# Joint transfers for blocks 2 and 3, a new order for the stages of blocks 2 to 5, and later float64 work, in a kernel for attention and two gated layers

## The chip, the core and the metric

The kernel runs on one core of one Trainium2 chip. The metric is the device time of one execution in microseconds, as the median of several runs. For the kernel before it is 1256.46 us over three runs (1255.62 to 1256.68).

## The reference

A chunked attention feeds a layer of four experts, and that feeds a gated layer. Everything arrives in float32, except the three matrices of the gated layer, which come in float64 (they were scaled with a float64 factor).

```python
scores = scale * np.matmul(q_c, k_c.transpose(0, 1, 2, 4, 3))   # B, H = 4, 8; chunks of 64 of 576; D = 64
scores = scores - np.max(scores, axis=-1, keepdims=True)
attn = np.exp(scores)
attn = attn / (np.sum(attn, axis=-1, keepdims=True) + 1e-09)
x = np.matmul(attn, v_c)                                        # -> 2304 tokens x 512
for e in range(4):                                              # first layer: w1 512 x 1024, w2 1024 x 512
    out += p[:, e:e + 1] * (np.maximum(x @ w1[e], 0.0) @ w2[e])
g, val = out @ w_gate, out @ w_val                              # second layer: 512 x 1536
return (silu(g) * val) @ w_out                                  # 1536 x 512
```

## The kernel before

**Tiling.** The 2304 tokens make 18 blocks of 128 tokens, and three passes of six blocks (two halves of three blocks, 384 tokens each). Attention makes blocks 0 to 5 before the first pass; blocks 6 to 17 are made beside the matmuls of that pass. Every product of the layers is done in a split form: an operand is a rounded high part (`h`) and the rest (`l`), and three matmuls add up h·h, h·l and l·h. A weight's high part is a copy on ScalarE (ACT), its low part a subtraction on GpSimd (POOL), both at L105 and L106 (tile `w`).

**Sets of products.** A *set* is a square of 256 columns of the first matrices; the first layer has 16 sets a pass, the second 12 a pass, 84 in all. A set is made with seven half-size products (`PRODUCTS`, a Strassen scheme) out of sums of weights and sums of inputs, six matmuls each (L538 to L540, 384 columns). The first three sets have no sums of inputs yet and are made as twelve *plain* products (`next_plain`, tiles `plz`, `plw`, `plx`) of twelve matmuls each. Between the products stand the matmuls of the second matrices (`layer2`, tile `y`, L587 to L591, 512 columns).

**Blocks 0 to 5.** Each block a goes through stages, here with the names of their tiles: scores `s` (L238, 16 matmuls), maximum and difference on VectorE (DVE, `att_soft`, tiles `mx` and `e`), the exponential on ACT (`att_exp`), transposes `et` (L264), the sums of a row (`att_sums`, tiles `hs`, `sm`, `rs`), the products with the values `av` (L300), their scaling into `e` on DVE (L307), transposes `xt` and the split of the result (`att_out`: two high parts and a full copy `x` on ACT, L323 and L325; two low parts, on POOL or, for the last block of a half, on DVE straight from the PSUM tile, L109). TensorE runs its instructions in the program's order, so a stage that is not ready holds up all that stands behind it.

**Loads.** Queries, keys and values are loaded with 128 partitions of 2 KB each. Keys and values go into block-diagonal tiles (`kbd`, `vbd`): a transfer of 64 partitions for either head half, the rest being zeros that DVE and POOL write at the start. Transfers are issued on the queue of SyncE (SP) and, for a few, of ACT (L213 to L223). Eight semaphores serve all these transfers in turn, so a transfer is issued only when the one eight places earlier has landed; SP issues in order.

**Sets that are made beside the work.** From set 18 on a list of tasks turns the float64 weights into float32 and splits them (`convert`, `make_set64`, `make_wo`; the seven splits of such a set are tile `w_made`), and makes the sums of inputs of the next pass (`x_sums`). After each product `run_tasks(2)` lets every running task go on until it says `WAIT` or `STEP`, with two `STEP`s at most. A conversion allows two raw tiles (`loads`):

```python
while loads[0] == RAWS: yield WAIT
loads[0] += 1
nc.sync.dma_start(raw..., src)          # L402, 4 WAITs later the arithmetic begins
...
nc.gpsimd.tensor_tensor(out=neg, in0=neg, in1=low, op=ALU.mult)          # L423
nc.gpsimd.tensor_tensor(out=top or dst, in0=top, in1=neg, op=ALU.add)    # L424
loads[0] -= 1
```

`later(d, f)` calls f d products later. The weights of a coming product are loaded (or made) six products ahead (`LEAD`, `load_w`, L386). The end of a pass of the first layer transposes its sums once more (`turn_x1`, tile `x1t`, copied by ACT at L627), in the PSUM tiles that `y` uses too.

Of the kernel before, what the change touches and what calls it, by code (L numbers as in the profile page):

```python
# [19 lines left out]
P = 128  # L20
# [51 lines left out]
def attention_moe_gated(  # L72
# [125 lines left out]
    def place(a):  # L198
        return a % 4 if a < BLOCKS else a % 2

    def next_in_place(a):

        return next((b for b in range(a + 1, NS) if place(b) == place(a)), None) if place(a) < 2 else None

    def att_load(a):
        q = (at_p if a < 2 or a >= BLOCKS - 2 else first_p).tile([P, NPAIR, P], F32, tag="q", name=f"q{a}", bufs=2)
        k = kbd[place(a)]

        for h in range(2):
            b = slice(64 * h, 64 * h + 64)  # L210
            queue = nc.scalar if a < 2 and h == 0 else nc.sync
            if a < 2:
                queue.dma_start(q[b], qt[a, b])  # L213
            elif h == 0:
                (nc.scalar if a < 4 else nc.sync).dma_start(q, qt[a])
            queue.dma_start(k[b, h].rearrange("p i c t -> p (i c t)"), kt[a, b].rearrange("p i t -> p (i t)"))
        att[a] = {"q": q, "k": k}

    def att_load_v(a):
        v = vbd[place(a)]  # L220
        for h in range(2):
            b = slice(64 * h, 64 * h + 64)
            (nc.scalar if a < 2 and h == 0 else nc.sync).dma_start(  # L223
                v[b, h].rearrange("p i c d -> p (i c d)"), vt[a, b].rearrange("p i c d -> p (i c d)")
            )
        att[a]["v"] = v

    def att_ps(name, where):
        pool, tag = where
# [403 lines left out]
    with tc.manual_schedule():  # L633
# [17 lines left out]
        for i in range(4):  # L651
            pool = at_p if i < 2 else first_p
            kbd.append(pool.tile([P, 2, NPAIR, 2, CH], F32, tag=f"k{i}", name=f"kbd{i}", bufs=1))
            vbd.append(pool.tile([P, 2, NPAIR, 2, D], F32, tag=f"v{i}", name=f"vbd{i}", bufs=1))
# [6 lines left out]
        for i in range(4):  # L661
            for t in (kbd[i], vbd[i]):
                for h in range(2):
                    (nc.vector if t is kbd[0] or t is kbd[1] else nc.gpsimd).memset(t[64 * h : 64 * h + 64, 1 - h], 0.0)
            if i == 2:
# [14 lines left out]
        def where():  # L680
            count[0] += 1
            return spare[count[0] % len(spare)]
# [26 lines left out]
        def stages(*some):  # L709
            for stage, a, *w in some:  # L710
                if 0 <= a < BLOCKS:
                    stage(a, *w)

        for i in range(-1, BLOCKS + 1):
            if i >= HALF + 1:
                next_plain()
            stages((att_values, i - 1, where()))
            stages((att_scores, i + 1, where()))  # L720
            if i == HALF:
                stages((att_out, i - 1, where()))
            if i == BLOCKS:
                next_plain()
            stages((att_turn, i, where()), (att_soft, i + 1), (att_sums, i))
            if i != HALF:
                stages((att_out, i - 1, where()))
            stages((att_exp, i + 1))
            if i == 1:
                fetch_w1(1)  # L730
            elif i == 2:
                w_plain(0, ORDER[:2])
            elif i == 3:
                w_plain(0, ORDER[2:])
                fetch_w1(2)
                shares()
            elif i == 4:
                w_plain(1, ORDER)
            elif i == 5:
                w_plain(2, ORDER[:2])  # L740
                first_cm.close()
                w2_p = ctx.enter_context(tc.tile_pool(name="w2", bufs=7, reuse_waits="tile"))
                fetch_w2(0, 0)
                fetch_w2(0, 1)
                first_sums(0)

        del raw1[0], raw1[1]
        now[0] = -10
# [114 lines left out]
        for o in order:  # L863
# [129 lines left out]
```

## Time and profile before

| | |
|---|---|
| median of three runs | 1256.46 us |
| the profiled execution | 1255.25 us, span 1253.5 us |
| TensorE matmuls busy | 1238.6 us (99%) |
| weight loads / VectorE / ScalarE / GpSimd busy | 1119.6 / 678.4 / 519.1 / 580.8 us |
| granted TensorE clock | 1.00 over the span |
| DMA | 328.40 MB, 262 GB/s on average |

Times in the rows count from the start of the span; 1.75 us of the profiled execution lie outside it. Engine names: PE is TensorE, PEld its weight loads, SPq and ACTq the transfers that SP and ACT issue. In a row of a timeline the bracket at its end says how long the engine was idle before the instruction and what ended that.

### The profile page before, as it was taken

How to read it: one execution, taken by the hardware profiler on the slowest of the kernel's cores; microseconds unless marked ns; L12 is line 12 of the kernel's file. 1: busy time of each engine (PE TensorE's matmuls, PEld its weight loads, DVE VectorE, ACT ScalarE, POOL GpSimd, SP SyncE). 2: the span in 40 equal slices, each digit the busy share in tenths (PEclk: the TensorE clock that was granted, in tenths of full speed). 3: DMA queues.
4: the chain of work that ended last, by engine and by line, in shares of the span. 5: the costliest groups of instructions: out<-in, count | busy, mean ns of one | idle time of the engine just before them, and what ended most of it. 6: DMA issues, size and time to landing. Idle time of an engine off the chain costs nothing.

```text
span 1253.5 us, 19769 instructions
## 1 busy us (share of the span) xinstructions
PE 1238.6 (99%) x6730; PEld 1119.6 (89%) x6730; DVE 678.4 (54%) x1115; ACT 519.1 (41%) x1114; POOL 580.8 (46%) x573
## 2 busy tenths in 40 slices
PE   7999999999999999999999999999999999999998
PEld 6888888899898988898998999999999999999997
DVE  5766666666555767665565663443345433543333
ACT  4454434445344444544543442343334333433331
POOL 5454434577445556545574461144456332442321
PEclk9999999999999999999999999999999999999999
DMA  8588787799798888988899886667967676577541
GB/s 228 168 277 277 265 273 234 249 329 342 258 350 310 304 302 336 325 314 304 290 354 345 290 298 232 240 226 241 314 205 280 223 244 186 200 249 245 179 140 51
DMA packets 170660, 328.40 MB, mean 262 GB/s; under 512 B 18224, under 2 KB 44080, under 8 KB 170560
## 3 DMA queue, kind: packets, MB, share of 16 engines
q1 hardware_dynamic: 169760, 325.79, 75.2%
q10 hardware_dynamic: 768, 1.31, 0.4%
q8 instruction: 54, 0.88, 0.3%
q14 instruction: 46, 0.38, 0.1%
q0 software_dynamic: 32, 0.04, 0.0%
HBM read 235.31 MB, written 91.75 MB: 261 GB/s over the span
## 4 chain that ended last, share of the span: by engine, by line
PE 90%; DMA 4%; POOL 2%; DVE 1%; ACT 1%; issue 1%; SPq 1%; DVEq 0%; POOLq 0%
PE y L587 14%; PE y L591 14%; PE y L589 14%; PE lx L538 9%; PE lx L540 8%; PE lx L539 8%; PE lz L538 4%; PE lz L540 4%; PE lz L539 4%; PE lw L538 2%; PE lw L540 2%; PE lw L539 2%; PE s L238 1%; PE av L300 1%; DMA w<-w_made 1%
## 5 line engine op out<-in xcount | busy, mean ns | idle before, releaser
L587 PE MATMUL y<-w,hh 128*128 128x512 f32 x792 | 312.3, 394 | 1.5 <-ACT acc L627 1.5
L591 PE MATMUL y<-w,hl 128*128 128x512 f32 x792 | 312.0, 394 | 0.0
L589 PE MATMUL y<-w,hh 128*128 128x512 f32 x792 | 310.8, 392 | 0.2 <-POOL w L106 0.2
L106 POOL TENSOR_TENSOR w<-raw,w 128x256 fp32r<-128x256 f32 (+1 forms) x192 | 189.5, 1000 | 212.2 <-ACT w L105 184.4
L591 PEld LDWEIGHTS y<-w,hl 128*128 128x128 f32 x792 | 148.6, 188 | 32.9 <-POOL hl L109 0.3
L587 PEld LDWEIGHTS y<-w,hh 128*128 128x128 f32 x792 | 148.9, 188 | 29.8 <-ACT acc L627 2.0
L589 PEld LDWEIGHTS y<-w,hh 128*128 128x128 f32 x792 | 148.8, 188 | 28.0 <-POOL w L106 0.6
L109 POOL TENSOR_TENSOR hl<-sg,hh 128x384 fp32r<-128x384 f32 x72 | 78.2, 1091 | 182.0 <-ACT hh L513 130.1
L495 ACT ACTIVATE hh<-sum_p 128x384 fp32r<-128x384 f32 x90 | 47.2, 525 | 230.2 <-DVE sum_p L526 230.1
L526 DVE TENSOR_TENSOR sum_p<-lx,p 128x384 f32<-128x384 f32 x81 | 45.2, 557 | 175.5 <-PE lx L540 174.3
L608 DVE SCALAR_TENSOR_TENSOR acc<-y,prob,acc 128x512 f32<-128x512 f32 x126 | 91.5, 744 | 79.5 <-PE y L591 79.4
L106 POOL TENSOR_TENSOR w_made<-raw,w_made 128x256 fp32r<-128x256 f32 x84 | 68.1, 819 | 83.1 <-ACT w_made L105 67.9
L105 ACT ACTIVATE w<-raw 128x256 fp32r<-128x256 f32 (+1 forms) x192 | 90.3, 488 | 7.3 <-DVE raw L370 2.6
L496 DVE SCALAR_TENSOR_TENSOR hl<-sum_p,hh 128x384 fp32r<-128x384 f32 x90 | 58.3, 647 | 60.1 <-ACT hh L495 60.1
L522 ACT COPY u<-lx 128x384 f32<-128x384 f32 x81 | 38.6, 477 | 92.6 <-PE lx L540 92.6
L513 ACT ACTIVATE hh<-sg 128x384 fp32r<-128x384 f32 x72 | 38.0, 528 | 67.5 <-DVE sg L510 67.5
L526 DVE TENSOR_TENSOR sum_p<-lw,p 128x384 f32<-128x384 f32 x81 | 44.9, 554 | 37.5 <-PE lw L540 32.5
L423 POOL TENSOR_TENSOR neg<-neg,raw 128x512 f32<-128x512 f32 x24 | 32.0, 1333 | 70.4 <-DVE neg L421 26.4
L538 PE MATMUL lw<-b21h,w 128*128 128x384 f32 x162 | 54.9, 339 | 1.2 <-DMA w<-w 1.2
L538 PE MATMUL lz<-t1h,w 128*128 128x384 f32 x162 | 55.2, 340 | 0.2 <-DVE hl L496 0.2
L538 PE MATMUL lx<-t3h,w 128*128 128x384 f32 x162 | 55.0, 340 | 0.0
L538 PE MATMUL lx<-t2h,w 128*128 128x384 f32 x162 | 55.0, 340 | 0.0
(235 smaller groups left out, 2826.7 us busy)
## 6 DMA issues: line engine op xcount, KB each, us to landing
w<-w SPq DMA_DIRECT2D x567, 256.0 KB, 5.1
w<-w SPq DMA_DIRECT2D x96, 512.0 KB, 6.1
w<-w_made SPq DMA_DIRECT2D x84, 256.0 KB, 5.9
raw<-w SPq DMA_DIRECT2D x19, 512.0 KB, 4.5
raw<-wo SPq DMA_DIRECT2D x36, 256.0 KB, 4.7
raw<-w SPq DMA_DIRECT2D x32, 256.0 KB, 4.3
sums<-x SPq DMA_DIRECT2D x40, 192.0 KB, 3.9
xt<-sums SPq DMA_DIRECT2D x40, 192.0 KB, 4.7
```

Of the source, the lines that this page charges most:

```text
L105: nc.scalar.activation(h, src, AF.Copy)
L106: (lo or nc.vector).tensor_tensor(out=l, in0=src, in1=h.bitcast(F32), op=ALU.subtract)
L109: (eng or nc.vector).tensor_tensor(out=o, in0=a, in1=b, op=ALU.subtract)
L496: nc.vector.scalar_tensor_tensor(out=l, in0=src, scalar=0.0, in1=h.bitcast(F32), op0=ALU.max, op1=ALU.subtract)
L526: nc.vector.tensor_tensor(out=t, in0=ps, in1=snap.pop(name), op=ALU.add)
L538: nc.tensor.matmul(ps, w[:, 0, c], xh[:, k], start=f, stop=False, skip_group_check=True)
L539: nc.tensor.matmul(ps, w[:, 0, c], xl[:, k], start=False, stop=False, skip_group_check=True)
L540: nc.tensor.matmul(ps, w[:, 1, c], xh[:, k], start=False, stop=e, skip_group_check=True)
L587: nc.tensor.matmul(y, hh[:, c], w[:, 0], start=(j == 0), stop=False)
L589: nc.tensor.matmul(y, hh[:, c], w[:, 1], start=False, stop=False)
L591: nc.tensor.matmul(y, hl[:, c], w[:, 0], start=False, stop=(j == 3))
L608: nc.vector.scalar_tensor_tensor(out=sum_, in0=y, scalar=p, in1=sum_, op0=ALU.mult, op1=ALU.add)
```

## The change

Six edits. (1) Queries, keys and values of blocks 2 and 3 lie in joint tiles `q23`, `k23`, `v23`; one transfer (queries) or two (keys, values) bring both blocks, and the first weights (`raw1_0`) are fetched behind them. (2) The stages of blocks 2 to 5 and the first four plain products are written out in a new order. (3) `att_out` of the last block of a half copies `x` after the two low parts and not before them. (4) A conversion gives its raw tile free one product later. (5) `x_sums` stores its sums three products later. (6) `run_tasks` is left out for the first four products of a pass's first set.

```diff
-            yield WAIT
+            for _ in range(4):
+                yield WAIT
             for i, o in enumerate(("b11", "b22", "b12", "b21")):
                 nc.sync.dma_start(xt_d[p][i, :, k], b[o])
...
+    def load_pair(both, src):
+        for h in range(2):
+            b = slice(64 * h, 64 * h + 64)
+            nc.sync.dma_start(
+                both[b, :, h].rearrange("p a i c t -> p a (i c t)"),
+                flat_pair(src[2:4, b]),
             )
...
             t = x_first[half, b] = acc_p.tile([P, KD, P], F32, tag="acc", name=f"x0_{a}")
-            nc.scalar.copy(t, ps)
             src, eng = (ps, nc.vector) if b == HALF - 1 else (t, nc.gpsimd)
+            if eng is nc.gpsimd:
+                nc.scalar.copy(t, ps)
             for i, (h, l) in enumerate(ops):
                 sub(l[:, :, r], src[:, 2 * i : 2 * i + 2], h[:, :, r].bitcast(F32), eng)
+            if eng is nc.vector:
+                nc.scalar.copy(t, ps)
...
+    def freed():
+        loads[0] -= 1
...
-        loads[0] -= 1
+        later(1, freed)
         return top
...
-        for a in range(4):
-            att_load(a)
-            if a > 0:
-                att_load_v(a - 1)
-            if a == 2:
-                fetch_w1(0)
-        att_load_v(3)
+        att_load(0)
+        att_load(1)
+        att_load_v(0)
+        nc.scalar.dma_start(q23.rearrange("p a i t -> p a (i t)"), flat_pair(qt[2:4]))
+        load_pair(k23, kt)
+        att_load_v(1)
+        load_pair(v23, vt)
+        for i in range(2):
+            att[2 + i] = {"q": q23[:, i], "k": kbd[2 + i], "v": vbd[2 + i]}
+        fetch_w1(0)
...
+        att_turn(3, where())
+        att_soft(4)
+        att_sums(3)
+        att_exp(4)
+        att_scores(5, where())
+        att_soft(5)
+        w_plain(0, ORDER[2:])
+        fetch_w1(2)
+        att_exp(5)
+        next_plain()
+        att_values(3, where())
+        turn(4)
+        w_plain(1, ORDER[:2])
+        next_plain()
+        att_out(3, where())
+        att_values(4, where())
+        turn(5)
+        w_plain(1, ORDER[2:])
+        shares()
+        next_plain()
+        att_out(4, where())
+        att_values(5, where())
...
-            if not (last_of_pass(n) or last_of_pass(n + 1) and i >= 5):
+            if not (last_of_pass(n) or last_of_pass(n - 1) and i < 4 or last_of_pass(n + 1) and i >= 5):
                 run_tasks(2)
```

On SP, at the very start, behind the first transfers of blocks 0 and 1 (the digit in a name is the block; `raw1_0` holds the first weights). Before:

```order
L223 DMA vbd0_191<-vt 64x512
L216 DMA kbd2_194<-kt 64x512 x2
L223 DMA vbd1_193<-vt 64x512
L360 DMA raw1_0_246<-w1 128x1024
L216 DMA kbd3_196<-kt 64x512 x2
L223 DMA vbd2_195<-vt 64x512 x2
L223 DMA vbd3_197<-vt 64x512 x2
L215 DMA q4_265<-qt 128x512
L216 DMA kbd0_190<-kt 64x512 x2
```

And now, in the same place:

```order
L225 DMA vbd0_191<-vt 64x512
L231 DMA k23_195<-kt 64x2x512 x2
L225 DMA vbd1_193<-vt 64x512
L231 DMA v23_196<-vt 64x2x512 x2
L374 DMA raw1_0_242<-w1 128x1024
L217 DMA q4_253<-qt 128x512
L218 DMA kbd0_190<-kt 64x512 x2
```

Four transfers fewer stand before those of block 4 (its keys go into `kbd0`), and on ACT's queue `q23` takes the place of two; with the eight semaphores in turn, the keys of block 4 now wait for transfers of `k23` and `vbd1`, and no longer for `raw1_0`.

On TensorE, from the transposes of block 3 on (a plain product is twelve rows, of which the first stands here). Before:

```order
L264 MATMUL et3_457<-ident_63,e3_394 128x128 x4
L538 MATMUL plz_0_0_0_487<-b11h_0_352,w_0_1_417 128x384
...
L300 MATMUL av3_504<-vbd3_197,et3_462 64x128 x8
L238 MATMUL s5_514<-kbd1_192,q5_283 64x128 x8
L264 MATMUL et4_527<-ident_63,e4_465 128x128 x4
L264 MATMUL xt3_543<-ident_63,e3_394 128x128 x4
...
L300 MATMUL av4_588<-vbd0_191,et4_532 64x128 x8
L264 MATMUL et5_600<-ident_63,e5_535 128x128 x4
L264 MATMUL xt4_612<-ident_63,e4_465 128x128 x4
...
L300 MATMUL av5_657<-vbd1_193,et5_605 64x128 x8
```

And now:

```order
L275 MATMUL et3_445<-ident_63,e3_382 128x128 x4
L249 MATMUL s5_462<-kbd1_192,q5_271 64x128 x8
L555 MATMUL plz_0_0_0_488<-b11h_0_340,w_0_1_405 128x384
...
L311 MATMUL av3_505<-v23_196,et3_450 64x128 x8
L275 MATMUL et4_515<-ident_63,e4_453 128x128 x4
...
L275 MATMUL xt3_550<-ident_63,e3_382 128x128 x4
L311 MATMUL av4_565<-vbd0_191,et4_520 64x128 x8
L275 MATMUL et5_577<-ident_63,e5_476 128x128 x4
...
L275 MATMUL xt4_617<-ident_63,e4_453 128x128 x4
L311 MATMUL av5_628<-vbd1_193,et5_582 64x128 x8
```

The scores of block 5 now come before the first plain product, and a plain product stands between the transposes `et` and `xt` of blocks 4 and 5.

On SP, in set 37 and 38 of the second pass, where `x_sums` stores into `xt_3` and two conversions fetch (`raw_4_1_1` and `raw_wo_9`; `w_38`, `w_39` are weights of coming products). Before:

```order
L386 DMA w_38_5_7550<-w_6_83 128x512
L402 DMA raw_4_1_1_7555<-wv 128x1024
L402 DMA raw_wo_9_7557<-wo 128x1024
L442 DMA w_24_101<-w_made_4_0_7_7517 128x512
L458 DMA w2_19_0_7573<-w2_12_117 128x1024
L386 DMA w_39_0_7575<-w_7_84 128x512
L178 DMA xt_3_74<-sums0_3_1_7398 128x384
L178 DMA xt_3_74<-sums1_3_1_7401 128x384
...
L442 DMA w_24_101<-w_made_4_0_3_7536 128x512
L386 DMA w_39_1_7613<-w_7_84 128x512
```

And now:

```order
L400 DMA w_38_4_7459<-w_6_83 128x512
L459 DMA w_23_100<-w_made_3_1_3_7404 128x512
L400 DMA w_38_5_7472<-w_6_83 128x512
L475 DMA w2_19_0_7491<-w2_12_117 128x1024
L400 DMA w_39_0_7493<-w_7_84 128x512
L400 DMA w_39_1_7530<-w_7_84 128x512
...
L400 DMA w_39_3_7601<-w_7_84 128x512
L179 DMA xt_3_74<-sums0_3_1_7366 128x384
L179 DMA xt_3_74<-sums1_3_1_7369 128x384
```

The two fetches and the four stores have left the place between `w_38_5` and `w_39_1`.

## Rows read from the trace of the kernel before

**Rows 1.** Page, busy time of each engine.
```profile
PE 1238.6 (99%) x6730; PEld 1119.6 (89%) x6730; DVE 678.4 (54%) x1115; ACT 519.1 (41%) x1114; POOL 580.8 (46%) x573
```

**Rows 2.** Windows: stretch, length, busy of each engine, PEclk, DMA share, GB/s.
```profile
0.00:46.00 46.00, 37.99 (x338) 33.07 (x339) 28.03 (x59) 22.08 (x51) 27.40 (x48) 1.00 0.75 206
46.00:570.00 524.00, 523.39 (x2908) 465.10 (x2907) 338.22 (x536) 235.78 (x528) 277.72 (x281) 1.00 0.83 293
570.00:600.00 30.00, 28.72 (x153) 26.03 (x152) 18.01 (x31) 13.81 (x31) 16.77 (x18) 1.00 0.89 308
600.00:680.00 80.00, 78.84 (x398) 70.90 (x397) 47.80 (x75) 33.45 (x73) 44.68 (x44) 1.00 0.94 337
680.00:1240.00 560.00, 560.00 (x2899) 516.80 (x2898) 243.49 (x412) 213.96 (x434) 214.18 (x186) 1.00 0.67 229
1240.00:1253.50 13.50, 9.67 (x43) 7.69 (x41) 2.83 (x5) 0.00 (x0) 0.00 (x0) 1.00 0.27 98
```

**Rows 3.** Waits of PE: who waited for whom, us, times, longest.
```profile
PE y L587 <- ACT acc L627: 1.5, 2, 1.3
...
PE lw L538 <- DMA w<-w: 1.2, 1, 1.2
```

**Rows 4.** Timeline of PE, 0 to 62 us: start, duration, instruction, idle before.
```profile
10.56 1.09 PE L300 MATMUL av<-vbd,et 128*64 128x128 f32 x16 [0.72 <-POOL hs L288]
11.56 1.09 PE L238 MATMUL s<-kbd,q 128*64 128x128 f32 x16
...
13.98 1.09 PE L300 MATMUL av<-vbd,et 128*64 128x128 f32 x16 [0.30 <-ACT et L275]
15.91 1.09 PE L238 MATMUL s<-kbd,q 128*64 128x128 f32 x16 [0.84 <-DMA kbd<-kt]
...
20.27 1.09 PE L238 MATMUL s<-kbd,q 128*64 128x128 f32 x16 [0.84 <-DMA kbd<-kt]
...
23.72 0.41 PE L539 MATMUL plz<-b11l,w 128*128 128x384 f32 x1 [0.87 <-DVE b11l L109]
...
33.61 0.66 PE L264 MATMUL xt<-ident,e 128*128 128x128 f32 x4 [0.85 <-DVE e L307]
```

**Rows 5.** Chain of waits: start, duration, step.
```profile
7.91 6.91 DMA raw<-w
...
15.35 4.67 DMA kbd<-kt
...
667.35 4.99 DMA w<-w
```

**Rows 6.** Transfers issued from 6.73 to 7.3 us: count, KB each, us to landing.
```profile
q<-qt ACTq DMA_DIRECT2D x1, 256.0 KB, 5.5
kbd<-kt SPq DMA_DIRECT2D x1, 128.0 KB, 5.1
```

**Rows 7.** Windows, 10 to 12 us.
```profile
10.00:12.00 2.00, 1.44 (x24) 1.35 (x26) 0.98 (x5) 0.99 (x2) 1.32 (x4) 1.00 1.06 252
```

**Rows 8.** Timeline of DVE, 23 to 30 us.
```profile
23.15 0.42 DVE L109 TENSOR_TENSOR b11l<-xt,b11h 128x256 fp32r<-128x256 f32 x1 [2.94 <-ACT x L325]
...
26.39 0.65 DVE L705 TENSOR_SCALAR prob_sum<-prob_sum 128x18 f32<-128x18 f32 x1
...
27.68 0.68 DVE L307 TENSOR_TENSOR e<-av,rs 128x512 f32<-128x512 f32 x1
```

**Rows 9.** Timeline of ACT, 576 to 593 us.
```profile
580.07 0.49 ACT L495 ACTIVATE hh<-lx 128x384 fp32r<-128x384 f32 x1 [2.58 <-PE lx L540]
...
583.63 1.07 ACT L627 COPY acc<-x1t 128x512 f32<-128x512 f32 x2
```

**Rows 10.** Timeline of SP's queue, 640 to 675 us: issue, duration, transfer.
```profile
661.52 0.33 SPq L402 DMA_DIRECT2D raw_wo<-wo  x1
...
663.35 3.24 SPq L178 DMA_DIRECT2D xt<-sums  x4
```

**Rows 11.** Waits of SP's queue over the whole span.
```profile
SPq L402 <- POOL neg L423: 73.4, 18, 9.3
```

More of the change, by code (lines that the diff above doesn't have):

```diff
@@ L203, in next_in_place, with flat @@
         return next((b for b in range(a + 1, NS) if place(b) == place(a)), None) if place(a) < 2 else None
+    def flat(x):
+        return x.rearrange("p i c t -> p (i c t)") if len(x.shape) == 4 else x.rearrange("p i t -> p (i t)")
     def att_load(a):
-        q = (at_p if a < 2 or a >= BLOCKS - 2 else first_p).tile([P, NPAIR, P], F32, tag="q", name=f"q{a}", bufs=2)
-        k = kbd[place(a)]
+        q = at_p.tile([P, NPAIR, P], F32, tag="q", name=f"q{a}", bufs=2)
         for h in range(2):
@@ L212, in att_load @@
             if a < 2:
-                queue.dma_start(q[b], qt[a, b])
+                queue.dma_start(flat(q[b]), flat(qt[a, b]))
             elif h == 0:
-                (nc.scalar if a < 4 else nc.sync).dma_start(q, qt[a])
-            queue.dma_start(k[b, h].rearrange("p i c t -> p (i c t)"), kt[a, b].rearrange("p i t -> p (i t)"))
-        att[a] = {"q": q, "k": k}
+                queue.dma_start(q, qt[a])
+            queue.dma_start(flat(kbd[place(a)][b, h]), flat(kt[a, b]))
+        att[a] = {"q": q, "k": kbd[place(a)]}
     def att_load_v(a):
@@ L222, in att_load_v, with flat_pair @@
             b = slice(64 * h, 64 * h + 64)
-            (nc.scalar if a < 2 and h == 0 else nc.sync).dma_start(
-                v[b, h].rearrange("p i c d -> p (i c d)"), vt[a, b].rearrange("p i c d -> p (i c d)")
-            )
-        att[a]["v"] = v
+            (nc.scalar if a < 2 and h == 0 else nc.sync).dma_start(flat(v[b, h]), flat(vt[a, b]))
+        att[a]["v"] = v
+    def load_pair(both, src):
[4 more added lines that the diff above has]
+                flat_pair(src[2:4, b]),
+            )
+    def flat_pair(x):
+        return x.rearrange("a p i t -> p a (i t)") if len(x.shape) == 4 else x.rearrange("a p i c t -> p a (i c t)")
     def att_ps(name, where):
@@ L650, in attention_moe_gated @@
         kbd, vbd = [], []
[L651 to L654, printed above, removed]
+        for i in range(2):
+            kbd.append(at_p.tile([P, 2, NPAIR, 2, CH], F32, tag=f"k{i}", name=f"kbd{i}", bufs=1))
+            vbd.append(at_p.tile([P, 2, NPAIR, 2, D], F32, tag=f"v{i}", name=f"vbd{i}", bufs=1))
+        q23 = first_p.tile([P, 2, NPAIR, P], F32, name="q23", bufs=1)
+        k23 = first_p.tile([P, 2, 2, NPAIR, 2, CH], F32, name="k23", bufs=1)
+        v23 = first_p.tile([P, 2, 2, NPAIR, 2, D], F32, name="v23", bufs=1)
+        for i in range(2):
+            kbd.append(k23[:, i])
+            vbd.append(v23[:, i])
         make_identity(nc, ident)
@@ L660, in attention_moe_gated @@
             nc.tensor.matmul(warm[:, :P], ident, ident, start=True, stop=True)
-        for i in range(4):
-            for t in (kbd[i], vbd[i]):
+        for i in range(2):
+            for eng, t in (nc.vector, kbd[i]), (nc.gpsimd, vbd[i]):
                 for h in range(2):
-                    (nc.vector if t is kbd[0] or t is kbd[1] else nc.gpsimd).memset(t[64 * h : 64 * h + 64, 1 - h], 0.0)
-            if i == 2:
-                nc.gpsimd.dma_start(prob, probs)
-        for a in range(4):
-            att_load(a)
-            if a > 0:
-                att_load_v(a - 1)
-            if a == 2:
-                fetch_w1(0)
-        att_load_v(3)
+                    eng.memset(t[64 * h : 64 * h + 64, 1 - h], 0.0)
+        for t in k23, v23:
+            for h in range(2):
+                nc.gpsimd.memset(t[64 * h : 64 * h + 64, :, 1 - h], 0.0)
+            if t is k23:
+                nc.gpsimd.dma_start(prob, probs)
+        att_load(0)
[5 more added lines that the diff above has]
+        load_pair(v23, vt)
+        for i in range(2):
+            att[2 + i] = {"q": q23[:, i], "k": kbd[2 + i], "v": vbd[2 + i]}
+        fetch_w1(0)
         spare = [(psA, "a"), (psX, "x"), (psY, "y")]
@@ L707, in shares, with turn @@
             nc.gpsimd.tensor_tensor(out=prob, in0=prob, in1=sm.unsqueeze(2).to_broadcast(prob.shape), op=ALU.mult)
[L709 to L728, printed above, removed]
+        def turn(a):
+            att_turn(a, where())
+            if a + 1 < HALF + 1:
+                att_soft(a + 1)
+            att_sums(a)
+        att_scores(0, where())
+        att_soft(0)
+        att_exp(0)
+        for i in range(HALF):
+            if i > 0:
+                att_values(i - 1, where())
+            att_scores(i + 1, where())
+            turn(i)
+            if i > 0:
+                att_out(i - 1, where())
+            att_exp(i + 1)
             if i == 1:
@@ L732, in attention_moe_gated @@
                 w_plain(0, ORDER[:2])
[L733 to L745, printed above, removed]
+        att_values(2, where())
+        att_scores(4, where())
+        att_out(2, where())
+        att_turn(3, where())
[20 more added lines that the diff above has]
+        att_values(5, where())
+        w_plain(2, ORDER[:2])
+        first_cm.close()
+        w2_p = ctx.enter_context(tc.tile_pool(name="w2", bufs=7, reuse_waits="tile"))
+        fetch_w2(0, 0)
+        fetch_w2(0, 1)
+        first_sums(0)
+        next_plain()
+        att_out(5, where())
         del raw1[0], raw1[1]
```

## The prediction

> **What bounds the kernel now.** I read the page's busy times first, then a table of windows, then the waits of TensorE, and only then single stretches. The reader is to see that TensorE is the bound nearly everywhere: it is busy for 1238.6 us of the span of 1253.5 [rows 1]. Since the change adds or removes no matmul, it can only win what is left, 14.9 us, and lose whatever new waits it makes. The windows say where these 14.9 us lie [rows 2]: 46.00 - 37.99 = 8.0 us in the first 46 us; 0.6 in the 524 us after that; 1.3 in the stretch 570 to 600; 1.2 in 600 to 680; nothing from 680 to 1240; 3.8 at the end, which no edit touches. The granted clock is 1.00 in every one of them. So there are three places to look at, and the first is the largest.
>
> In the first place the timeline of TensorE gives each wait [rows 4]. The scores of blocks 3 and 4 (at 15.91 and 20.27) wait 0.84 us each for their keys; the first plain product stops for 0.87 us at 23.72 for the low part `b11l`; the transposes `xt` of block 4 wait 0.85 us at 33.61 for the scaled `e`. Together 3.40 us. The rest of the 8.0 (start of the engine, blocks 0 and 1, the 0.72 and 0.30 before the two `av` shown) belongs to stages that keep their order. These idle times leave out a little, because the last matmul ahead of a stop is counted as busy until its modelled end: between 10.56 and 11.56 one `av` hands over to scores in 1.00 us without a wait, while from 13.98 to 15.91 it takes 1.93, which is 0.93 lost where 0.84 is shown. With about 0.1 for each of the four I take 3.8 us as what the order could give.
>
> The second place is one wait of 1.3 us of `y` for the copies `acc` of `x1t`, and the third one wait of 1.2 us of `lw` for a weight transfer [rows 3].
>
> **The change part by part.**
>
> *Keys of block 4.* Their transfer was issued at 15.35 (its other half 14.84) and took 4.67 us, so the scores could start at 20.27; it had stood behind `raw1_0`, issued at 7.91 and landed 6.91 us later, at 14.82 [rows 5]. In the new order that semaphore is one of `k23` and `vbd1`, which land before 14 us by the argument below. The keys are then issued some 2 us earlier, and the 0.84 goes. Gain about 0.95.
>
> *Keys of block 3.* They come with those of block 2 and have landed when block 2's scores start. Gain about 0.95, but not for nothing: the scores of block 2 now need all of `q23` and `k23`, 512 KB more in front of them than before. Before, the second half of block 2's keys was issued shortly before 6.73 us (its transfer is the one still being issued there) and took 5.1 us, so it landed at 11.3, just in time for 11.56 [rows 4, 6]. The queries of block 3 (256 KB, issued right behind, 5.5 us) were largely moved alongside already, so what is new in front is block 3's keys, 256 KB. At the 252 GB/s of that stretch, in which the DMA engines are full (share 1.06) [rows 7], these are 1.04 us: landing at about 12.3, scores at 12.35 instead of 11.56. Cost 0.8. Bounds: 0 below (the two queues shared so that nothing comes later; no gain, since `av` holds TensorE until 11.56 in the present order), and above 512 KB at 252 GB/s, 2.1 us. I take 0.8, as the queries' own row says that half of the extra had been moved.
>
> The Trainium skill, "DMA: Bandwidth & Descriptors", section Measured, advises to batch transfers, since small ones reach a lower rate (64 KB 138 GB/s, 1 MB 341 GB/s in its table); by that the joint transfers of 256 and 512 KB would be quicker than the halves and the 0.8 would vanish. The trace speaks against it here: with pieces of 128 and 256 KB the engines are already full [rows 7].
>
> *The low parts of block 2 and of block 5.* Before, DVE waited 2.94 us for ACT's full copy `x`, and began at 23.15 [rows 8]. Now the copy comes after the two low parts, so they start some 0.5 us earlier after the transposes; and the scores of block 5, 1.0 us by the spacing above, stand between them and the plain product. Both together cover the 0.87. Gain about 1.0. The copy and the transposed `et` of block 3 behind it on ACT come some 0.8 us later than they would (two low parts at 0.42); who needs them is `av` of block 3, which now has the scores and a whole plain product in front of it, and is covered.
>
> *`xt` of block 4.* With a plain product between `et` and `xt` (twelve matmuls, 2.1 us by the rows' spacing of 0.17) the 0.85 is covered. Gain 0.95. But the same order puts the maximum and the difference of block 5 (two DVE instructions of about 0.68 each) ahead of the scaling of block 3, in place of the three small ones on `prob` (0.65 the longest, about 1.1 together) [rows 8], and ACT's exponential of block 5 waits for that difference and stands ahead of the copy `hh` of the first plain product, on which `hl` and then the scaling wait on DVE. Counted through from the transposes of block 2: the scaling of block 3 ends about 7.8 us later, and TensorE arrives at `xt` of block 3 after about 7.7 (0.5 + 0.5 + 1.0 + 2.1 + 1.0 + 0.5 + 2.1). A new wait of 0.3 us there, between 0 and 1.5 (an exponential, `hh`, `hl` and a scaling wholly in the open).
>
> Start together: 3.8 - 0.8 - 0.3 = 2.7 us less.
>
> *The weight transfer at 667.35.* It took 4.99 us [rows 5] and was late since SP had stood: at 661.52 for a raw tile that POOL gave free late, and at 663.35 for four stores, 3.24 us [rows 10]. Edits 4 and 5 take both kinds of wait out of SP's way: a fetch comes a product later, about 2.2 us, against a mean wait of 73.4 / 18 = 4.1 us for POOL in the whole span [rows 11], and by the order the weight of that product (`w_39_1`) is now issued ahead of four stores and two fetches. Gain 1.2, between 0 (another weight late in its place) and 1.3.
>
> *The pause at a pass's begin.* It covers the first four products of set 32. The wait of `y` for `acc` comes in set 33, where the copy stands behind that set's `p`, so the pause does not reach it. What delays that copy is ACT's queue, busy without a break from 580.07 until the copies at 583.63 [rows 9]; in the new order two splits and the three ACT steps of a conversion still stand there ahead of them. I take nothing, between a loss of 0.5 and a gain of 1.3.
>
> The conversions end some products later, but ended long before they are needed: POOL's work of that kind is not part of any wait of TensorE after 680 [rows 2]. Cost nothing; if this cover were gone, a late weight costs about 1.2 a time, as the row at 667 shows.
>
> Sum: 2.7 + 1.2 + 0 = 3.9 us less than the profiled execution's own 1255.25, that is 1251.35. The median shown is 1.2 above that execution, so as a median I forecast 1252.5.
>
> **The rivals.**
>
> *A: the joint transfers cost as much as they bring.* If `q23` and `k23` land at 13.4 (all 512 KB in front), block 2's scores come 1.85 us late, the waits of block 3 are gone anyway, and block 5's keys, now wanted earlier, are late too by up to 0.5. The start then gives 3.8 - 1.85 - 0.5 - 0.3 = 1.15, all together 2.3: 1254.1. For it: the engines are full from 5 us on [rows 7]. Against: a part of the extra had been moved by 11.3.
>
> *B: everything works.* No new wait at the start, because larger transfers move at a higher rate or the queues share better than I reckon, and ACT's copies in set 33 happen to come in time: 3.8 + 1.2 + 1.3 = 6.3, so 1250.2. (The first of these is the rule of the Trainium skill cited above.) For it: ACT's queue there does change. Against: the steps in front of the copies are as many as before.
>
> *C: slower, by SP.* The float64 fetches are not fewer, only placed elsewhere between the weight loads. A weight is loaded six products ahead, about 13.4 us (six of about 2.2), and lands in 5: SP may lag 8.4 us behind. The longest single wait of a fetch for POOL is 9.3 [rows 11]. If the longer list after the pause makes such waits fall together, each product's weight behind them is about 1.2 late; from four such places on the gain is gone, and with six the time is 1256.46 - 2.7 + 6 x 1.2 = 1261. Against: POOL has 44.68 of 80 us to do in the worst stretch [rows 2], and each fetch asks later for the same tile.
>
> *D: the mid-part only changes places.* The late weight at 672 goes and another comes, or two: 2.7 + 1.2 - 2 x 1.2 = 1.5 less, 1255.0, within what can be told from no change.
>
> **How the numbers follow.** About 0.2%, 2.5 us, is what a measurement of this kernel can tell from no change; so faster means below 1253.9 and slower above 1259.0. Chances: the forecast 0.57 (its own range 1250.8 to 1254.0), A 0.15, B 0.11, C 0.04, D 0.13. Faster: 0.54 of the forecast, all of B, 0.07 of A and 0.03 of D, 0.75. Slower: C and a little for a mishap not named, 0.05. Same: 0.20. The range reaches from just under B's time to just beyond D's: 1250.0 to 1255.4.
>
> **What would show it.** In the profile after: scores of block 2 at about 12.3 instead of 11.56; those of blocks 3 and 4 with no wait for `k` or `kbd`, at about 15.8 and 19.2; the first plain product without a stop; `xt` of block 4 without one, a short one at `xt` of block 3; the idle time of the first 46 us down from 8.0 to about 5.3. No wait of `lw` for `w` between 600 and 680. Still a wait of `y` for `acc` of about 1.3 where the second pass's sums are turned. I am wrong if block 2's scores start after 13 us, if new waits for `w` come up between 340 and 780, or if the wait for `acc` is gone.

## The result and the profile after

The changed kernel takes 1272.55 us (median of four runs, 1272.32 to 1273.75), the kernel before on the same chip 1256.06: a ratio of 1.0133, 95% interval 1.0115 to 1.015. It is slower by 16.5 us, where 4 less had been forecast. The forecast was wrong, on the other side.

The page gives the busy times, as in [rows 1]:

```profile
PE 1247.0 (98%) x6730; PEld 1126.1 (89%) x6730; DVE 671.5 (53%) x1115; ACT 519.7 (41%) x1114; POOL 576.9 (45%) x569
```

TensorE runs the same 6730 instructions, but is busy for 8.4 us longer, and the span grew by 17.0 (1270.5). Work that takes longer without being more work points to the clock. The windows, with the columns of [rows 2]:

```profile
0.00:46.00 46.00, 39.45 (x335) 34.55 (x336) 28.49 (x59) 22.30 (x51) 27.07 (x43) 0.96 0.77 203
46.00:570.00 524.00, 523.47 (x2911) 465.48 (x2910) 325.96 (x527) 228.75 (x513) 266.70 (x270) 1.00 0.84 290
570.00:600.00 30.00, 27.72 (x147) 24.99 (x146) 17.98 (x27) 14.72 (x32) 10.96 (x11) 1.00 0.72 240
600.00:680.00 80.00, 80.00 (x406) 72.38 (x405) 49.49 (x79) 34.41 (x75) 49.06 (x51) 1.00 0.93 334
680.00:940.00 260.00, 260.00 (x1338) 238.11 (x1337) 122.39 (x207) 105.26 (x217) 114.42 (x108) 1.00 0.78 272
940.00:1000.00 60.00, 49.56 (x225) 44.28 (x224) 23.03 (x35) 18.48 (x35) 21.83 (x16) 0.89 0.54 184
1000.00:1257.00 257.00, 257.00 (x1337) 238.55 (x1337) 101.30 (x179) 95.75 (x194) 86.89 (x72) 1.00 0.60 194
```

The same window of the kernel before:

```profile
940.00:1000.00 60.00, 60.00 (x316) 55.94 (x315) 28.66 (x46) 24.16 (x47) 27.43 (x20) 1.00 0.72 251
```

The reader sees the whole loss in one row: from 940 to 1000 TensorE gets through 225 matmuls instead of 316, and the granted clock is 0.89 where it had been 1.00. Up to there the change is level: the same product (`lx` with `t2h`) starts at 948.10 before and at 947.88 now, 0.2 us earlier; 17.0 at the end make 17.2 us lost between.

The waits of TensorE, longest first (us, times, longest), to be held against [rows 3]:

```profile
PE lx L555 <- ACT t2h L105: 4.8, 1, 4.8
PE lz L555 <- DMA w<-w: 3.6, 1, 3.6
PE y L604 <- ACT acc L644: 2.5, 2, 2.3
PE lx L555 <- DMA w<-w: 2.0, 1, 2.0
```

The first, second and fourth lie in that window, at 957.01, 974.14 and 968.24: 10.3 us. Behind the stops at 957 and 974 the clock is at its lower level, behind the shorter one at 968 it is not. Two short windows of the same kernel:

```profile
955.00:960.00 5.00, 2.99 (x9) 3.02 (x10) 2.69 (x5) 1.47 (x2) 0.61 (x1) 0.62 0.90 290
975.00:980.00 5.00, 5.00 (x14) 3.84 (x12) 1.57 (x1) 1.22 (x3) 2.44 (x2) 0.50 0.55 166
```

A clock of 0.50 is 1.2 of 2.4 GHz. A product's matmuls then follow each other every 0.32 us instead of 0.17, those of `y` every 0.43 instead of 0.23: 18 of the first kind behind the stop at 957 and 6 with 9 of the second behind that at 974 cost 18 x 0.15 + 6 x 0.15 + 9 x 0.20 = 5.4 us. With the 10.3 this is 15.7 of the 17.2. Of the rest about 0.5 lies ahead of the three stops, where the last matmul is counted as busy until its modelled end, and about 1.0 in the first matmul behind each stop and in short gaps up to 983. The Trainium skill ("TensorE: Matmul & The Clock Gate", section "Loop structure matters more than you think") shows a loop with a long wait for a transfer before every matmul as the bad case, in which the engine goes cold; this trace agrees for single stops of 4.80 and 3.57 us with late transfers behind them: 0.62 and 0.50.

What made TensorE wait stands in SP's queue (issue, duration, transfer):

```profile
922.77 3.08 SPq L169 DMA_DIRECT2D sums<-x  x4
...
931.77 15.62 SPq L186 DMA_DIRECT2D xraw_b<-x  x2
953.04 0.32 SPq L186 DMA_DIRECT2D xraw_t<-xt  x1
...
958.01 0.32 SPq L186 DMA_DIRECT2D xraw_t<-xt  x1
...
964.25 0.32 SPq L186 DMA_DIRECT2D xraw_t<-xt  x1
964.62 0.90 SPq L400 DMA_DIRECT2D w<-w  x2
...
980.42 2.87 SPq L179 DMA_DIRECT2D xt<-sums  x4
```

and in the chain of waits (start, duration, step):

```profile
946.10 0.96 DVE b11l L106
947.08 3.10 DMA xraw_b<-x
950.26 0.85 ACT b21h L105
951.18 1.84 POOL b21l L106
953.04 3.09 DMA xraw_t<-xt
956.15 0.85 ACT t2h L105
...
964.62 3.48 DMA w<-w
```

The next pass's inputs come one at a time: fetch, high part, low part, and only then the next fetch, 5 to 6 us apart. In the kernel before the stores stand ahead of the fetches, the first three fetches go out within 1.4 us, and TensorE waits for none of them:

```profile
930.03 5.88 SPq L178 DMA_DIRECT2D xt<-sums  x4
...
938.83 0.90 SPq L185 DMA_DIRECT2D xraw_b<-x  x2
939.77 0.47 SPq L185 DMA_DIRECT2D xraw_t<-xt  x1
```

In the changed kernel SP, which issues in order, stood for 15.62 us with the weights behind it. The reason is in the code: `x_sums` and `x_fetch` take their tiles from one pool `xt` of three buffers. `x_sums` holds two from its loads (922.77) to its stores (980.42), and the stores now come behind the fetches. This is edit 5. The last `x_sums` is begun at the first product of set 56, and from there the list of tasks runs after 20 products before it pauses for the pass's end. With one WAIT the second half's stores come out at the 15th, with three at the 19th, with four at the 21st, so behind the pause and the fetches: by this count one product too late.

At the start block 2's scores wait for the joint keys, and the clock falls here too (TensorE's timeline; the first `et` behind the scores takes 1.12 us, that of block 3 0.66):

```profile
11.09 1.09 PE L311 MATMUL av<-vbd,et 128*64 128x128 f32 x16 [0.72 <-POOL hs L299]
13.85 1.74 PE L249 MATMUL s<-k,q 128*64 128x128 f32 x16 [1.67 <-DMA k<-kt]
...
18.39 1.04 PE L249 MATMUL s<-k,q 128*64 128x128 f32 x16
...
21.70 1.07 PE L249 MATMUL s<-kbd,q 128*64 128x128 f32 x16
...
24.04 1.09 PE L249 MATMUL s<-kbd,q 128*64 128x128 f32 x16
...
31.14 0.66 PE L275 MATMUL xt<-ident,e 128*128 128x128 f32 x4
```

The window behind the late scores:

```profile
15.00:20.00 5.00, 5.00 (x52) 4.17 (x49) 3.16 (x7) 2.25 (x5) 1.26 (x2) 0.74 1.05 272
```

What was late is the transfer itself. The second half of the joint keys was issued at 6.24, that of block 2's own keys in the kernel before at 6.29, and took 7.48 us where that took 5.1 [rows 6]:

```profile
6.24 7.48 DMA k<-kt
```

The scores of blocks 3, 4 and 5 (18.39, 21.70, 24.04) have no wait, as forecast, and `xt` of block 3 (31.14) has none either, where a short one had been expected. Those of block 2 come at 13.85 instead of 11.56 [rows 4]; 0.53 of these 2.29 us were gone before, since the `av` ahead of them starts at 11.09 instead of 10.56. The first `y` starts at 55.25, before at 54.73: the start lost 0.5 instead of gaining 2.7.

### The profile page after: what moved, and what is told of

Read it like the earlier page. It is cut to its first block, busy times and chain, and to the rows that moved or that the text cites. A ratio compares the mean times of both kernels' runs of the same rounds, so it can differ in the third digit from the quotient of the medians.

```text
span 1270.5 us, 19731 instructions
## 1 busy us (share of the span) xinstructions
PE 1247.0 (98%) x6730; PEld 1126.1 (89%) x6730; DVE 671.5 (53%) x1115; ACT 519.7 (41%) x1114; POOL 576.9 (45%) x569
## 4 chain that ended last, share of the span: by engine, by line
PE 93%; DMA 3%; DVE 1%; ACT 1%; issue 1%; POOL 1%; SPq 0%; DVEq 0%; ACTq 0%; POOLq 0%
PE y L604 14%; PE y L608 14%; PE y L606 14%; PE lx L555 9%; PE lx L557 9%; PE lx L556 9%; PE lz L555 4%; PE lz L557 4%; PE lz L556 4%; PE lw L555 2%; PE lw L557 2%; PE lw L556 2%; PE av L311 1%; PE s L249 1%; DMA xraw_b<-x 1%; PE et L275 1%
## 5 line engine op out<-in xcount | busy, mean ns | idle before, releaser
L555 PE MATMUL lx<-t4h,w 128*128 128x384 f32 x162 | 54.9, 339 | 2.0 <-DMA w<-w 2.0
L555 PE MATMUL lz<-b22h,w 128*128 128x384 f32 x162 | 55.4, 342 | 0.0
```

What stands on the lines that cost most here:

```text
L555: nc.tensor.matmul(ps, w[:, 0, c], xh[:, k], start=f, stop=False, skip_group_check=True)
```

## The experiments

Theory 1: edit 5 holds two of three buffers over the end of a pass, and everything between 948 and 1000 follows from that. Its rivals: the order on SP by itself (2), the pause of edit 6 (3), the start (4).

**Buffers of its own for the last `x_sums`**, every instruction in its place:

```diff
-                t = xt_p.tile([P, 2, TT], F32, tag="xt", name=f"sums{i}_{p}_{k}")
+                t = (xs_p if p == 5 else xt_p).tile([P, 2, TT], F32, tag="xt", name=f"sums{i}_{p}_{k}")
...
+                xs_p = ctx.enter_context(tc.tile_pool(name="xs5", bufs=2, side="right"))
```

> The changed kernel with one thing other: the last `x_sums` (that of the third pass of the second layer) takes its tiles from two buffers of its own instead of from the three that it shares with `x_fetch`. Every instruction of every engine stands in the same order as in the changed kernel. Theory 1 (the late stores keep two of three buffers while `x_fetch` wants them, so its tiles come one at a time, and SP stands with the weights behind it): the 17.3 us lost between 948 and 1000 go, 1255 to 1256.5, and SP's queue no longer shows 15.62 us at the fetch of `xraw_b`. Theory 2 (the new order of SP itself: stores and weight loads behind the fetches): the order is the same, so 1268 to 1273. Theory 3 (the pause at a pass's begin delays work that TensorE needs): also unchanged, about 1272.

Measured: 1256.08 us, ratio to before 1.0003 (0.999 to 1.0017). The window of the loss, in this kernel:

```profile
940.00:1000.00 60.00, 60.00 (x316) 56.01 (x315) 28.78 (x46) 25.27 (x51) 29.34 (x22) 1.00 0.68 235
```

and SP's queue:

```profile
935.67 0.96 SPq L186 DMA_DIRECT2D xraw_b<-x  x2
937.46 0.32 SPq L186 DMA_DIRECT2D xraw_t<-xt  x1
...
960.71 2.35 SPq L400 DMA_DIRECT2D w<-w  x5
963.11 3.58 SPq L179 DMA_DIRECT2D xt<-sums  x4
```

The four stores still stand behind the fetches and behind the same five weights, and TensorE has no idle time in this window. So neither the order nor the pause lost the time: the buffers did. Theories 2 and 3 fall as the cause. What is left of the change is level with the kernel before.

**Three WAITs instead of four.**

```diff
-            for _ in range(4):
+            for _ in range(3):
                 yield WAIT
```

> The changed kernel with three WAITs in `x_sums` instead of four, nothing else. By the counting of tasks the stores of the last `x_sums` then come out two products earlier, just ahead of the first three fetches of the next pass. Theory 1 (buffers held over the boundary): 1255 to 1257, the loss between 948 and 1000 gone, the rest of the trace as in the changed kernel (first `y` still at about 55.2, wait for `acc` still 2.3). Theory 4 (the loss comes mainly from the start, where block 2's scores came at 13.85 and the granted clock fell): over 1265, since the start is not touched.

Measured: 1254.17 us, ratio 0.9978 (0.9962 to 0.9993). The stores (931.77) now stand ahead of the fetches (938.33), and the stop is gone by this road too; theory 4 falls. By the count one product earlier would have been enough; that was not run. One part of the expectation was wrong: the wait of `y` for `acc` did not stay at 2.3, it fell to 0.2 (see below). The twelve runs lie far apart, 1251.12 to 1261.37. In the three quickest the mean granted clock is 1.000, in the three slowest 0.996 to 0.997. That fits a clock that falls at the start in some executions and not in others, but only one of these runs has a trace. Joint transfers are not the only source: the kernel before, on the same chip, went from 1254.63 to 1259.97 over 23 runs, with mean clocks down to 0.996.

**Four WAITs alone, in the kernel before.**

```diff
-            yield WAIT
+            for _ in range(4):
+                yield WAIT
```

> The kernel before with four WAITs in `x_sums` instead of one, nothing else: no pause at the pass's begin, old start, raw tiles given free as before. Theory 1: the stores again stand behind all seven fetches of that pass, the same stops of TensorE come, and the time is 1271.5 to 1273.5 (16 to 17 us more, up to 1.2 less for the weight at 667). Theory 3 (the pause does it) or theory 4 (the start does it): 1255 to 1257.

Measured: 1283.33 us, ratio 1.0207 (1.0188 to 1.0226). Edit 5 needs none of the others to do its harm. It does more than expected: between 948 and 1000 some 21 us go, and 3.4 more at two stops that the changed kernel doesn't have, for a weight at 378.85 (1.07) and for `hl` at 416.31 (2.32).

**Without the pause at a pass's begin.**

```diff
-if not (last_of_pass(n) or last_of_pass(n - 1) and i < 4 or last_of_pass(n + 1) and i >= 5):
+if not (last_of_pass(n) or last_of_pass(n + 1) and i >= 5):
```

> The changed kernel without edit 6, the pause of the tasks over the first four products of a pass. Theory 1: the stores of the last `x_sums` then come right behind the seventh fetch, some products earlier than in the changed kernel but still behind all fetches, so 1271 to 1273.5. Theory 3 (the pause does it): 1260 or less. Beside it: the wait of `y` for `acc` near 583, 2.3 us with the pause, shows whether the pause is what made it 1.0 longer (then 1.3 here) or not (then still about 2.3).

Measured: 1276.61 us, ratio 1.0163 (1.0141 to 1.0184), above the expected range. The loss at the boundary is larger without edit 6, 22.2 us in the profiled execution (0.5 ahead at 948, 21.7 behind at the end); one more stop stands there, 3.41 us at 986.02. In this kernel the four stores (977.25) stand ahead of the weights of the next products (980.50), with the pause behind five of them; that this is the reason is argued, not shown. The wait of `y` for `acc` is 0.2, neither of the two values that had been expected.

The start, theory S1: the joint transfers hold block 2 back, the new order of stages gains.

**Separate transfers in the new order** (three WAITs).

```diff
-        nc.scalar.dma_start(q23.rearrange("p a i t -> p a (i t)"), flat_pair(qt[2:4]))
-        load_pair(k23, kt)
-        att_load_v(1)
-        load_pair(v23, vt)
...
-        fetch_w1(0)
+        for a in range(4):
+            att_load(a)
+            if a > 0:
+                att_load_v(a - 1)
+            if a == 2:
+                fetch_w1(0)
+        att_load_v(3)
```

> The changed kernel with three WAITs in `x_sums` (1254.2 measured), and with edit 1 undone: keys, queries and values of blocks 2 and 3 in the separate tiles and transfers of the kernel before, `raw1_0` again behind those of block 2; the new order of stages stays. Theory S1 (the joint transfers hold block 2 back, the new order itself gains): scores of block 2 at about 11.6 instead of 15.3, no stretch at half clock before 25 us, first `y` at about 53 (56.4 with joint transfers, 54.7 in the kernel before); 1250.5 to 1252. Theory S2 (the new order itself loses, by its waits on ACT and DVE): first `y` at 54.7 or later, 1254 or more.

Measured: 1251.44 us (1250.35 to 1252.47), ratio 0.9955 (0.9941 to 0.997): faster than both kernels, and the eight runs lie within 2.1 us. The interval overlaps that of the joint transfers with three WAITs, so the times alone do not part these two; the timelines do. TensorE's timeline:

```profile
12.28 1.07 PE L239 MATMUL s<-kbd,q 128*64 128x128 f32 x16
...
16.37 1.09 PE L239 MATMUL s<-kbd,q 128*64 128x128 f32 x16 [0.61 <-DMA vbd<-vt]
...
21.63 1.09 PE L239 MATMUL s<-kbd,q 128*64 128x128 f32 x16 [1.75 <-DMA kbd<-kt]
```

and the window from 15 to 20:

```profile
15.00:20.00 5.00, 3.98 (x55) 3.12 (x50) 3.04 (x9) 3.04 (x8) 2.71 (x5) 1.00 1.01 253
```

Block 2 waits no more, the clock stays at 1.00. Its first `y`, at 54.86, is later than expected (53) and where S2 had it, since the scores of blocks 3 and 4 still wait, 0.61 and 1.75. In three later kernels with the same start it came at 53.32 to 53.72: in one of them these waits were 0 and 0.70, in the two others `av` of block 0 came 0.4 to 0.8 earlier (11.01 and 10.57 instead of 11.38).

**The first weights behind all keys and values.**

```diff
-            if a == 2:
-                fetch_w1(0)
         att_load_v(3)
+        fetch_w1(0)
```

> As the run with separate transfers, but `raw1_0` is fetched after the values of block 3 instead of between the transfers of blocks 2 and 3. Theory S1: the keys of blocks 3 and 4 come earlier, their scores wait no more, 0.5 to 1.5 below the run with separate transfers, 1249.5 to 1251.5. Rival: the weights of the first plain products are now the late ones, first `y` no earlier, same time as the run with separate transfers or up to 1 more.

Measured: 1251.68 us, ratio 0.9956 (0.994 to 0.9972), no difference. The wait of block 3's scores goes, that of block 4's grows from 1.75 to 2.38, and the first `y` comes at 54.72. The rival's time holds, though not by its reason: late are the keys of block 4, not the first weights.

**Joint transfers alone, in the old order** (edit 1 in the kernel before, one WAIT).

```diff
-        for a in range(4):
-            att_load(a)
...
+        nc.scalar.dma_start(q23.rearrange("p a i t -> p a (i t)"), flat_pair(qt[2:4]))
+        load_pair(k23, kt)
+        att_load_v(1)
+        load_pair(v23, vt)
...
+        fetch_w1(0)
```

> The kernel before with edit 1 alone: joint transfers for blocks 2 and 3, `raw1_0` behind them, old order of stages, one WAIT. Theory S1: scores of block 2 at 13.8 to 15.5 and a stretch at half clock behind them, while the waits of the scores of blocks 3 and 4 for their keys (0.84 each) go: first `y` at 55 to 56.5, 1256.5 to 1258.5. Theory S3 (joint transfers are as good as separate ones, and the late scores come from something in the new order): scores of block 2 at 11.6 to 12.4, 1255 to 1256.

Measured: 1258.94 us, ratio 1.0016 (1.0002 to 1.003), a little above the expected range. The scores of block 2:

```profile
14.05 1.74 PE L248 MATMUL s<-k,q 128*64 128x128 f32 x16 [1.96 <-DMA k<-kt]
```

and the window behind them:

```profile
15.00:20.00 5.00, 5.00 (x52) 4.17 (x49) 2.95 (x7) 2.25 (x5) 1.05 (x2) 0.72 1.05 280
```

The first `y` comes at 56.66 instead of 54.73. So the joint transfers lose about 2 us by themselves and S3 falls. (The late weight near 670 is still there without the other edits, 1.7 us.)

**Work that fills the wait for block 2's keys** (three WAITs, joint transfers).

```diff
+        for i in range(14 if a == 2 else 0):
+            nc.tensor.matmul(ps[:, 0:2].rearrange("p h k -> p (h k)"), ident, ident, start=True, stop=True)
```

> The changed kernel with three WAITs, and 14 more products of the identity with itself ahead of the scores of block 2 (into the same bank, which the scores then overwrite), some 1.7 us of work that keeps TensorE busy while it would wait for the keys. Theory K (a part of the start's loss is the granted clock, which falls behind that wait): the clock in the window from 15 to 20 us is 1.00 instead of 0.74 or so, 1.2 to 1.8 us come back, 1252.4 to 1253.2. Rival: the wait itself is all, the time stays at 1254.2 or rises by up to 0.4.

Measured: 1253.45 us (1252.73 to 1254.44), ratio 0.997 (0.9959 to 0.9982). The filling and the scores of block 2:

```profile
11.52 3.39 PE L248 MATMUL s<-ident 128*128 128x128 f32 x28
14.99 1.09 PE L252 MATMUL s<-k,q 128*64 128x128 f32 x16
```

and the window behind them:

```profile
15.00:20.00 5.00, 4.70 (x62) 4.12 (x63) 3.22 (x7) 2.15 (x5) 1.52 (x3) 1.00 1.06 262
```

The clock is kept, as theory K has it. The filling took 3.39 us and not 1.7, and just covered the wait: the second half of the keys, issued at 6.45, landed 8.4 us later, at 14.85. From the start of block 2's scores to the first `y` (54.98) it is 39.99 us here, against 41.13 with three WAITs and 41.40 in the changed kernel: by estimate 1.1 to 1.4 us are the clock's share. In the time this is not shown: the medians, 1254.17 and 1253.45, come from two chips, and their ratios are not apart by their intervals. The runs lie within 1.7 us instead of 10, but on the chip of this run the kernel before, without joint transfers, went from 1254.34 to 1262.41, and separate transfers in the new order stayed within 2.1 without any filling; so the narrow spread does not tell what the filling does.

**Queries and keys of block 4 ahead of the values and of `raw1_0`** (separate transfers).

```diff
         att_scores(0, where())
+        att_load_v(2)
+        fetch_w1(0)
+        att_load_v(3)
```

> As the run with separate transfers (1251.44 measured), but the queries and keys of block 4 are issued right behind the keys of block 3, ahead of the values of blocks 2 and 3 and of `raw1_0`: the transfers then stand in the order in which they are wanted. Theory N (what is left at the start is the order of the transfers): the wait of block 4's scores for their keys (1.75) goes, first `y` at 53.2 instead of 54.9, 1249.6 to 1250.6. Rival (the DMA engines are full until 25 us, share 1.0, so what one transfer gains another loses): values, `raw1_0` or the keys of block 5 are late instead, 1251 to 1252.

Measured: 1252.78 us, ratio 0.9968 (0.9956 to 0.9981). The rival holds, at a little more than its time: the scores of block 4 start at 19.02 without a wait, and those of block 5 wait 2.05 us instead (23.29), with a clock of 0.89 from 20 to 25; the first `y` comes at 55.80. What one transfer gains another loses here, with the DMA engines full (share 1.03 from 15 to 20 and 1.04 from 20 to 25).

The last three undo one of the other edits in the kernel with separate transfers.

**One WAIT again.**

```diff
-            for _ in range(3):
-                yield WAIT
+            yield WAIT
```

> The run with separate transfers (three WAITs, 1251.44) with one WAIT, so edit 5 is undone and edits 2, 3, 4 and 6 stay. If the WAITs are what took the late weight near 670 away, a wait of `lw` or `lx` for `w` of about 1.2 is back between 600 and 680, and the time is 1252.2 to 1253; if edit 4 alone did it, there is none and the time stays at 1251.4.

Measured: 1253.97 us, ratio 0.9978 (0.9968 to 0.9987). No wait between 600 and 680 (80.00 busy), so the late weight goes without edit 5 too. Edit 4 was meant to do that, but edits 2, 3 and 6 are in this kernel as well, and no run has edit 4 alone. Edit 5 alone was enough (79.91 in the kernel before with four WAITs).

**Raw tiles free at once** (edit 4 undone).

```diff
-        later(1, freed)
+        freed()
```

> The run with separate transfers (1251.44) with edit 4 undone: a conversion gives its raw tile free at once and not one product later. If edit 4 is what took the late weight near 670 away, a wait for `w` of about 1.2 comes back (there or in another place between 300 and 680), 1252.2 to 1255; if not, 1251.4. The kernel before with four WAITs alone, where tiles are also given free at once, had such waits at 378.85 (1.07) and a wait of 2.32 for `hl` at 416.31.

Measured: 1256.01 us, ratio 0.9996 (0.9987 to 1.0006), apart from the 0.9955 with edit 4. The weight near 670 is in time here as well; what comes back is spread: `y` waits 1.3 for `hl` (between 680 and 940) and 1.0 for `acc`, and one product 0.5 for a weight.

**No pause.**

```diff
-            if not (last_of_pass(n) or last_of_pass(n - 1) and i < 4 or last_of_pass(n + 1) and i >= 5):
+            if not (last_of_pass(n) or last_of_pass(n + 1) and i >= 5):
```

> The run with separate transfers (1251.44) with edit 6 undone: tasks run on over the first four products of a pass. By the prediction the pause is worth nothing: 1251 to 1252, and the wait of `y` for `acc` near 583 stays at 0.2. Rival (the pause keeps ACT free for the copies `acc` in the second pass): that wait comes back with 1 to 2.3 us, 1252.5 to 1253.7.

Measured: 1253.57 us, ratio 0.9977 (0.9968 to 0.9986). The wait for `acc` is back at 1.0. These intervals touch that of the run with separate transfers (to 0.997), so the worth of edits 5 and 6 in it, some 2 us each, is not settled.

## Why the prediction was wrong

**The failed step is edit 5**, "the weight transfer at 667.35" with its gain of 1.2. Four stores leave SP's way there, and the weight is in time, as said. But the edit was weighed in that one place, and its cost elsewhere put at nothing. Every `x_sums` stores later, a store that comes later gives its tile free later, and the pool that the tile is from was not looked up. In the program's order the last stores now stand behind the first fetches of the coming pass. It cost 17.2 us, at 948 to 1000, outside the stretch (340 to 780) in which the prediction would have looked for late weights. Rival C came nearest, with SP behind and weights late for 1261 at 4 in 100, but it looked for the delay at the float64 fetches; there it was not.

**The joint transfers** were priced at 0.8 with 2.1 as the upper bound: block 2's scores at 12.35, at most 13.4. They came at 13.85 in the changed kernel, and between 14.05 and 15.31 in the four other kernels with joint transfers and no filling. Two things were missing. The scores need the last byte of both joint transfers, and the later half of the keys took 7.48 us where the sum had about 6.1 (5.1 and the 1.04 for the new bytes); that the queries and values under way beside them are the reason is argued, not shown. And the clock, which the sum left at 1.00, fell to 0.74, for 1.1 to 1.4 us by the run with the filling. I had named scores after 13 us as a sign of being wrong, and so they were. Rival B's rule, that larger transfers move at a higher rate, does not help here: 256 KB in 7.48 us is more per microsecond than 128 KB in 5.1, but block 2 now waits for block 3's bytes too.

**The waits that should go went**: those of blocks 3 and 4 for keys, of the plain product for `b11l`, of `xt` of block 4. The 0.3 that I had added at `xt` of block 3 was not there, but short waits came that the sum had not: 0.25 at `xt` of block 2 (23.02), 0.38 and 0.19 for the weights of a later plain product (42.18, 42.99). With separate transfers and three WAITs the kernel takes 5.0 us less than before by the medians and 2.8 by the profiled executions, against 3.9 forecast for edits 1 to 6 together. That this is near is partly luck: the wait for `acc`, which the sum had at nothing, gives 1.0 of it, while the keys of block 4 still wait and the first `y` of that execution is no earlier than before. What spoiled the change were edit 5's four WAITs and, for some 2 us, edit 1.

**The pause** was taken as nothing, with 0.5 as the largest loss. The wait for `acc` grew from 1.3 to 2.3 in the changed kernel. ACT's timeline shows why: the three steps of a conversion had slid right ahead of the two copies.

```profile
582.72 0.63 ACT L429 ACTIVATE neg_wo<-top_wo 128x512 f32<-128x512 f32 x1 [0.61 <-DVE top_wo L427]
583.38 0.63 ACT L430 ACTIVATE top_wo<-top_wo 128x512 f32<-128x512 f32 x1
583.92 0.65 ACT L432 ACTIVATE raw_wo<-raw_wo 128x512 f32<-128x512 uint32 x1
...
584.83 1.07 ACT L644 COPY acc<-x1t 128x512 f32<-128x512 f32 x2
```

With three WAITs the same steps stand at 581.00, ahead of `hh`, and the wait is 0.2. Without the pause it is 0.2 with four WAITs and 1.0 with three (and separate transfers). So no single edit decides it; that it hangs on where the list of tasks happens to be by then is argued from these runs, not shown.

**Conversions that end later** were taken as free. No run speaks against that: without edit 4, which puts them off, the kernel with separate transfers is slower (0.9996 against 0.9955).

## What to carry to other kernels

When a store is put off, look up which pool its tile is from and who takes the next tile of it, and count to the places where the list pauses: stores at the 21st product instead of the 19th cost over 17 us. A joint transfer makes its first user wait for the last byte of all, so it pays only where the first user is not the one that waits. And a stop of TensorE is to be priced with the stretch at half clock that may follow it: here 5.4 us on top of 10.3.

## What had not been expected of the hardware

The granted clock fell behind a wait of 1.67 us at the start (0.74 from 15 to 20 us) and behind stops of 4.8 and 3.6 (0.62, 0.50). The length of a single stop does not decide: the stop of 1.75 at 21.63 in the kernel with separate transfers, that of 2.38 at 21.46 with the first weights behind the values, and that of 1.97 at 968.24 in the changed kernel left the clock of their windows (20 to 25 twice, 965 to 970) at 1.00. Even the same stop can go either way: `y` waits 2.3 us for `acc` in the changed kernel and in the one with buffers of its own, with the same order of instructions, and the clock of 570 to 600 is 1.00 in the first and 0.94 in the second. Work of no use in place of the wait kept the clock, 1.00 from 15 to 20 us, where the five kernels with joint transfers and no filling have 0.66 to 0.76.
